# A 64-row score product run on 128 rows, with zero-padded copies of q, in an attention, gated-MLP and experts kernel

## The chip, the cores and the metric

The kernel runs on one core of one Trainium2 chip. The metric is the device time of one execution in microseconds (us); the median of three runs before the change is 1014.93 us (1014.54 to 1016.13). A core has a matrix engine (PE, with its weight loads listed apart as PEld), a vector engine (DVE), a scalar engine (ACT), a general engine (POOL) and an engine that here only issues DMA transfers (SP). Each works through its own instructions in order and waits on semaphores for the others.

## The reference

Three layers follow one another, on 8 batches of 576 tokens and a width of 512: an attention with pooled keys, a gated MLP with a spatial mixing, and four experts with a causal attention each, of which the two best per token are added up. The change is in the third layer, which per batch and expert computes:

```python
for e in range(E):                       # 4 experts, head size 64
    q = x @ wq[e]; k = x @ wk[e]; v = x @ wv[e]
    scores = scale * (q @ k.transpose(0, 2, 1))
    scores = np.where(causal, -1000000000.0, scores)
    scores = scores - scores.max(-1, keepdims=True)
    a = np.exp(scores)
    a /= a.sum(-1, keepdims=True) + 1e-09
    ye = a @ v @ wo[e]
    ...                                  # added with the gate's weight
```

## The kernel before, in words

**Precision.** Matrix products run in a reduced 32-bit format (F32R). To keep accuracy, an operand is split into a high part, which that format holds, and a low part, which is the rest; a product is the sum of high by high, low by high and high by low.

**Phases.** Class PhaseA runs the first two layers, batch by batch, until about 596 us of the trace; class PhaseB runs the experts from there to the end. PhaseB takes the four experts as two pairs per batch, p = 0 and p = 1, and I call the stretch of one pair a first half and a second half of the batch. One batch takes 50.6 us in the middle of the phase. Within a pair there are nine units, u = 0 to 8, in the order of QT (L598): unit 0 is the last 64 tokens of both experts together (e = 2), units 1 to 4 are the query blocks 3, 2, 1, 0 of the pair's first expert, and units 5 to 8 those of the second. Because of the causal mask their scores are 512, 384, 256 and 128 columns wide.

**One unit.** score() (L799) computes the scores in a PSUM bank; a DVE instruction applies the mask and takes the extremum (L825); ACT takes the exponential (L828); DVE makes the reciprocal of the sum (L839, L840); POOL or DVE scales the row (L844); PE transposes it (L870, in trans); ACT and DVE copy the transpose into high and low parts (L874, L875); av() multiplies by v (L890). The loop of run() (L943 on) emits score of unit k, scale of unit k - 1, some filling work, and the transposes of unit k - 3 (LAG = 3). The filling work is listed by unit in FILL, FIRSTF and LASTF: the next projections of q and k (proj, L691, with put_q and put_k), of v (vproj), loads of x, and the output products of the batch before (outp, L912 to L914). This code order sets the order on PE.

**The score products.** put_q (L704) lays q out so that one product does two thirds of the sum: qs[:, e] has the high part of expert e in one half of the 128 partitions and the low part in the other half, and kd (written by four DMAs per pair, L734) has the high part of k in both halves. L823 multiplies these on 128 rows. The third term, high q by low k, runs on the 64 rows of expert e alone:

```python
nc.tensor.matmul(o, qs[:, e, 128 * i:n], kd[:, e, :n], start=True, stop=False)                # L823
nc.tensor.matmul(o, qs[hi(e), e, 128 * i:n], kl[hi(e), :n], start=False, stop=True)           # L824
```

kl holds the low part of k, of the first expert in partitions 0 to 63 and of the second in 64 to 127. Unit 0 does the same third term on 128 rows, with qd, a matrix that is zero outside two diagonal blocks (L813).

**Order and buffers.** The tile framework derives all waits from reads and writes of the tiles, and orders the instructions of each engine. q and k have two sets of buffers, taken in turn by pair. All of PhaseB's loads, stores and copies by DMA are issued by SP in one order.

Of the kernel before, what the change touches and what calls it, by code (L numbers as in the profile page):

```python
# [8 lines left out]
F32 = mybir.dt.float32  # L9
F32R = mybir.dt.float32r  # L10
# [32 lines left out]
class PhaseA:  # L43
# [35 lines left out]
    def consts(self):  # L79
        nc, c = self.nc, self.c  # L80
        self.ident = c.tile([128, 128], F32, name="ident")
        make_identity(nc, self.ident)
        self.cm = c.tile([128, 8], F32, name="cm")
        nc.scalar.dma_start(self.cm, self.ins["cm"])
        self.kbd, self.vhi, self.vlo, self.vl1, self.vl2 = [], [], [], [], []
        for i in range(1):
            for n, sh, dt in (("kbd", [128, NP, 144], F32), ("vhi", [128, NP, 128], F32R), ("vlo", [128, NP, 128], F32R)):
                t = c.tile(sh, dt, name=f"{n}{i}")
                nc.gpsimd.memset(t.bitcast(F32) if dt == F32R else t, 0.0)
                getattr(self, n).append(t)  # L90
        self.mhalf = c.tile([128, 2], F32, name="mhalf")
        nc.gpsimd.memset(self.mhalf, -0.5)
        warm = c.tile([128, 2], F32, tag="wl", name="warm", bufs=2)
        nc.scalar.activation(warm, self.mhalf, AF.Exp)
        self.vn2 = c.tile([128, 512], F32R, name="vn2")
        nc.gpsimd.memset(self.vn2.bitcast(F32), 0.0)
        nc.gpsimd.memset(self.vn2[64:66].bitcast(F32), 1.0)
# [515 lines left out]
class PhaseB:  # L613
# [23 lines left out]
    def consts(self):  # L637
        nc, c, w = self.nc, self.c, self.w
        wt = [c.tile([128, 4112], F32R, tag="wi", name=n, bufs=2) for n in ("wqh", "wql")]
        self.wq = [t[:, :3088].rearrange("p (k n) -> p k n", k=4) for t in wt]  # L640
        self.wo = [t[:, 3088:].rearrange("p (k n) -> p k n", k=2) for t in wt]
        self.mk = c.tile([128, 640], F32, tag="kbd0", name="mk")
        nc.gpsimd.memset(self.mk, 0.0)
        nc.gpsimd.affine_select(self.mk[:, 448:576], self.mk[:, 448:576], pattern=[[-1, 128]], compare_op=OP.is_ge,
                                fill=NEG, base=0, channel_multiplier=1)
        for h in range(2):
            r = slice(64 * h, 64 * h + 64)
            nc.gpsimd.affine_select(self.mk[r, 576:], self.mk[r, 576:], pattern=[[-1, 64]], compare_op=OP.is_ge,
                                    fill=NEG, base=0, channel_multiplier=1)
        self.ml = bass.AP(tensor=self.mk.tensor, offset=self.mk.offset, ap=[list(self.mk.ap[0]), [192, 4], [1, 64]])  # L650
        self.tri = c.tile([128, 4, 4], F32, tag="st", name="tri", bufs=3)
        nc.gpsimd.memset(self.tri, 0.0)
        for e in range(1, 4):
            nc.gpsimd.memset(self.tri[:, e, :e], 1.0)
        warm = c.tile([128, 2], F32, tag="wl", name="warm", bufs=2)
        nc.scalar.activation(warm, self.ident[:, :2], AF.Exp)
        self.qs, self.lg = [], []
        for i in range(2):
            a = c.tile([128, 2048], F32R, tag="wo", name=f"qs{i}", bufs=2)
            t = a[:, :1280].rearrange("p (e n) -> p e n", e=2)  # L660
            nc.gpsimd.memset(t[:, 0, S:].bitcast(F32), 0.0)
            nc.gpsimd.memset(t[:, 1, 512:S].bitcast(F32), 0.0)
            d = a[:, 1280:1408]
            nc.gpsimd.memset(d.bitcast(F32), 0.0)
            self.qs.append((t, d, a[:, 1408:1984]))
        self.pr = c.tile([128, 5, S], F32, tag="pv", name="pr", bufs=2)
        self.sc = c.tile([128, 5, S], F32, tag="pv", name="scr", bufs=2)
        self.vts = [c.tile([128, 5, S], F32R, tag="ws", name=f"vt{i}", bufs=2) for i in range(2)]
        for i in range(2):
            t = c.tile([128, 5, 4], F32, name=f"lg{i}")  # L670
            nc.gpsimd.memset(t, 0.0)
            self.lg.append(t)
# [31 lines left out]
    def put_q(self, b, p, ps, h, s):  # L704
        nc = self.nc
        t, qd, _ = self.qs[(2 * b + p) % 2]
        A, C = slice(0, 64), slice(64, 128)
        n = HS if h == 0 else 512 - HS
        o = [(t[:, 1, h * HS:h * HS + n], ps[:, :n])]
        if h:  # L710
            o.append((t[:, 1, S:], ps[:, n:]))
        nc.scalar.activation(t[A, 0, s], ps[A], AF.Copy)
        for d, x in o:
            nc.scalar.activation(d[C], x[C], AF.Copy)
        nc.vector.tensor_sub(t[C, 0, s], ps[A], t[A, 0, s].bitcast(F32))
        for d, x in o:
            nc.vector.tensor_sub(d[A], x[C], d[C].bitcast(F32))
        if h:
            for e, r in enumerate((A, C)):
                nc.scalar.activation(qd[r, 64 * e:64 * e + 64], ps[r, n:], AF.Copy)  # L720
            self.QK["q", b, p] = (t, qd)

    def put_k(self, b, p, ps, h, s):
        nc, w = self.nc, self.w
# [74 lines left out]
    def score(self, b, p, u):  # L799
        nc, w = self.nc, self.w  # L800
        i, e = QT[u]
        qs, qd = self.QK["q", b, p]
        kd, kl = self.QK["k", b, p]
        hi = lambda e: slice(64 * e, 64 * e + 64)
        st = w.tile([128, 8], F32, name="sm", bufs=4)
        pt = self.pr[:, (18 * b + 9 * p + u) % 5]
        if e == 2:
            parts = []
            for s in (slice(0, 320), slice(320, S)):
                o = self.bank("s4")[:, :s.stop - s.start]  # L810
                nc.tensor.matmul(o, qs[:, 0, 512:], kd[:, 0, s], start=True, stop=False)
                nc.tensor.matmul(o, qs[:, 1, 512:], kd[:, 1, s], start=False, stop=False)
                nc.tensor.matmul(o, qd, kl[:, s], start=False, stop=True)  # L813
                parts.append((o, s))
            o = parts[1][0].rearrange("p (a n) -> p a n", a=4)
            nc.vector.tensor_tensor_reduce(o, o, self.ml, -0.125, BIG, OP.add, OP.min, st[:, 4:5])
            o = parts[0][0]
            nc.vector.tensor_tensor_reduce(o, o, self.mk[:, 0:1].to_broadcast([128, 320]), -0.125, st[:, 4:5],
                                           OP.add, OP.min, st[:, 0:1])
        else:  # L820
            n = 128 * i + 128
            o = self.bank("s")[:, :n]
            nc.tensor.matmul(o, qs[:, e, 128 * i:n], kd[:, e, :n], start=True, stop=False)  # L823
            nc.tensor.matmul(o, qs[hi(e), e, 128 * i:n], kl[hi(e), :n], start=False, stop=True)  # L824
            nc.vector.tensor_tensor_reduce(o, o, self.mk[:, 576 - n:576], -0.125, BIG, OP.add, OP.min, st[:, 0:1])  # L825
            parts = [(o, slice(0, n))]
        for j, (o, s) in enumerate(parts):
            nc.scalar.activation(pt[:, s], o, AF.Exp, bias=st[:, 0:1], scale=-1.0, accum_out=st[:, 1 + 4 * j:2 + 4 * j])  # L828
        self.U[b, p, u] = (pt, st)
# [170 lines left out]
```

## Time and profile before

| | us |
|---|---|
| median of three runs | 1014.93 |
| profiled execution, its time | 1014.54 |
| its span, from the first to the last instruction | 1012.8 |
| PE busy over the span | 955.0 (94%), 6488 products |
| DVE busy | 720.9 (71%) |
| ACT busy | 516.2 (51%) |
| POOL busy | 490.5 (48%) |
| L823, 128 products | 279 to 562 ns each in the record, median 404 |
| L824, 128 products | 322 to 579 ns each in the record, median 439 |

How to read it: consecutive products overlap in the records, since a product's record runs from its start until its last result is out. What a product costs PE is the step from its start to the start of the next one, and that is read from a timeline, not from the mean duration. The share of busy time is an average over a phase that has stretches of different kinds; so the rows below take single half batches and single instructions.

### The profile page before, as it was taken

What the parts mean: (1) busy time and instruction counts of PE and PEld (TensorE: products, weight loads), DVE (VectorE), ACT (ScalarE), POOL (GpSimd) and SP (SyncE); (2) the same over time, 40 slices, a digit from 0 to 9 for tenths busy, and PEclk for the clock granted to TensorE, in tenths of its full rate; (3) what the DMA queues carried; (4) which work ended last, traced back from release to release, by engine and by line L of the source; (5) the groups of instructions that cost most, each with busy time, mean ns of one, the idle gap of its engine ahead of it and who ended that gap; (6) DMA issues with size and microseconds to landing.
All of it is one profiled execution on the core that took longest, in us unless ns stands there. A gap on an engine that the chain in (4) does not pass through costs nothing.

```text
span 1012.8 us, 18277 instructions
## 1 busy us (share of the span) xinstructions
PE 955.0 (94%) x6488; PEld 871.6 (86%) x6488; DVE 720.9 (71%) x1901; ACT 516.2 (51%) x1291; POOL 490.5 (48%) x666
## 2 busy tenths in 40 slices
PE   4577899999999999999999998999999999999998
PEld 3466889989999899899998997989898989898987
DVE  6998747657477575674775238896969696969685
ACT  5575334243243342432433415766666666767676
POOL 6863638459377483692773603142424242424221
PEclk9589999999999999999999997999999999999999
DMA  9421302202213023032131122131313131312111
GB/s 328 175 98 45 124 36 79 104 23 72 111 34 125 36 78 115 11 95 89 40 111 38 37 67 71 28 106 36 107 36 106 37 106 37 106 37 71 36 48 71
DMA packets 35258, 78.72 MB, mean 78 GB/s; under 512 B 4448, under 2 KB 10592, under 8 KB 34272
## 3 DMA queue, kind: packets, MB, share of 16 engines
q1 hardware_dynamic: 35024, 77.55, 24.0%
q8 instruction: 52, 0.85, 0.4%
q14 instruction: 38, 0.31, 0.1%
q10 hardware_dynamic: 144, 0.00, 0.0%
HBM read 49.23 MB, written 18.87 MB: 67 GB/s over the span
## 4 chain that ended last, share of the span: by engine, by line
PE 68%; DVE 19%; ACT 4%; POOL 4%; issue 3%; DMA 1%; SPq 0%; POOLq 0%; DVEq 0%; ACTq 0%
PE pj L699 4%; PE av L890 4%; PE op L445 4%; PE t L870 3%; PE op L446 3%; PE op L447 3%; PE pj L701 3%; PE pj L700 3%; PE s L824 3%; PE sp L420 3%; PE sp L422 3%; PE sp L421 3%; PE sc L230 3%; DVE vnl L390 2%; DVE vnh L392 2%
## 5 line engine op out<-in xcount | busy, mean ns | idle before, releaser
L844 POOL TENSOR_SCALAR pr<-pr,sm,gw 128x128 f32<-128x128 f32 (+3 forms) x119 | 79.3, 667 | 175.6 <-DVE sm L840 125.5
L828 ACT ACTIVATE pr<-s,sm 128x256 f32<-128x256 f32 (+4 forms) x160 | 83.0, 520 | 35.4 <-DVE sm L825 17.5
L332 POOL TENSOR_TENSOR xu<-x 128x576 f32<-128x576 f32 x28 | 39.2, 1435 | 98.2 <-DVE x L327 85.4
L446 PE MATMUL op<-g,woh 128*128 128x288 f32 x256 | 76.7, 301 | 4.2 <-POOL g L433 3.8
L420 PE MATMUL sp<-wsh,vnh 128*128 128x288 f32 x256 | 78.3, 306 | 1.6 <-ACT vnh L388 1.6
L404 PE MATMUL up<-x,wih 128*128 128x288 f32 x256 | 76.9, 301 | 2.4 <-ACT vg L364 2.3
L699 PE MATMUL pj<-xbh,wqh 128*128 128x288 f32 x256 | 78.8, 308 | 0.0
L445 PE MATMUL op<-g,woh 128*128 128x288 f32 x256 | 78.3, 309 | 0.0
L421 PE MATMUL sp<-wsh,vnl 128*128 128x288 f32 x256 | 76.1, 297 | 0.0
L422 PE MATMUL sp<-wsl,vnh 128*128 128x288 f32 x256 | 75.9, 297 | 0.0
L406 PE MATMUL up<-x,wil 128*128 128x288 f32 x256 | 75.7, 296 | 0.0
L700 PE MATMUL pj<-xbl,wqh 128*128 128x288 f32 x256 | 75.4, 294 | 0.0
L701 PE MATMUL pj<-xbh,wql 128*128 128x288 f32 x256 | 75.3, 294 | 0.0
L405 PE MATMUL up<-x,wih 128*128 128x288 f32 x256 | 75.1, 293 | 0.0
L447 PE MATMUL op<-g,wol 128*128 128x288 f32 x256 | 74.9, 297 | 0.0
L825 DVE CUSTOM_DVE_ANT_0 s<-s,mk 128x512 f32<-128x512 f32 (+3 forms) x128 | 62.4, 488 | 6.9 <-PE s L824 6.7
L282 ACT ACTIVATE pth<-tr 128x640 fp32r<-128x640 f32 (+1 forms) x40 | 26.2, 655 | 78.5 <-PE tr L281 68.9
L870 PE MATMUL t<-ident,pr 128*128 128x128 f32 x320 | 60.9, 290 | 4.7 <-DVE pr L844 3.0
L875 DVE TENSOR_TENSOR pbl<-t,pbh 128x512 fp32r<-128x512 f32 (+3 forms) x128 | 60.7, 484 | 3.9 <-ACT pbh L874 1.9
L230 PE MATMUL sc<-kbd,qt 128*128 128x144 f32 (+1 forms) x320 | 49.7, 301 | 11.5 <-DMA qt<-q_in 9.2
L874 ACT ACTIVATE pbh<-t 128x512 fp32r<-128x512 f32 (+3 forms) x128 | 53.5, 440 | 10.4 <-PE t L870 8.7
L361 PE MATMUL vp<-wih,x 128*128 128x512 f32 x128 | 52.0, 406 | 6.3 <-ACT wih L128 5.0
(237 smaller groups left out, 3398.4 us busy)
## 6 DMA issues: line engine op xcount, KB each, us to landing
kraw<-k_in SPq DMA_DIRECT2D x16, 576.0 KB, 3.8
x<-x SPq DMA_DIRECT2D x32, 288.0 KB, 2.1
xb<-x SPq DMA_DIRECT2D x32, 288.0 KB, 2.9
kd<-scr SPq DMA_DIRECT2D x64, 144.0 KB, 2.5
out<-o SPq DMA_DIRECT2D x32, 288.0 KB, 2.2
vraw<-v_in SPq DMA_DIRECT2D x16, 512.0 KB, 4.1
qt<-q_in SPq DMA_DIRECT2D x7, 1152.0 KB, 6.9
st<-w_in_in SPq DMA_DIRECT2D x8, 512.0 KB, 8.5
```

What stands on the lines that cost most here:

```text
L230: nc.tensor.matmul(ps[:m, p // 2, (p % 2) * 144:(p % 2) * 144 + 144], qt[:, p, o:o + m], kbd[:, p, :], start=p % 2 == 0, stop=True, skip_g ...
L420: nc.tensor.matmul(o, vh[:, k, c], self.ws[0][:, k, s], start=k == 0, stop=False)
L421: nc.tensor.matmul(o, vl[:, k, c], self.ws[0][:, k, s], start=False, stop=False)
L422: nc.tensor.matmul(o, vh[:, k, c], self.ws[1][:, k, s], start=False, stop=False)
L445: nc.tensor.matmul(o, self.wo[0][:, k, c], gh[:, s], start=k == 0, stop=False)
L446: nc.tensor.matmul(o, self.wo[0][:, k, c], gl[:, s], start=False, stop=False)
L447: nc.tensor.matmul(o, self.wo[1][:, k, c], gh[:, s], start=False, stop=k == 3)
L699: nc.tensor.matmul(ps, self.wq[0][:, kc, c], xh[:, s], start=kc == 0, stop=False)
L700: nc.tensor.matmul(ps, self.wq[0][:, kc, c], xl[:, s], start=False, stop=False)
L701: nc.tensor.matmul(ps, self.wq[1][:, kc, c], xh[:, s], start=False, stop=kc == 3)
L828: nc.scalar.activation(pt[:, s], o, AF.Exp, bias=st[:, 0:1], scale=-1.0, accum_out=st[:, 1 + 4 * j:2 + 4 * j])
L870: nc.tensor.transpose(ps[:, j], pt[:, 128 * j:128 * j + 128], self.ident)
```

## The change

Four tiles qz of 128 partitions by 512 columns are added, two for each of the two buffer sets, in the space of PhaseA's constants vhi0, vlo0, vn2 and gln. One half of each (64 partitions) is set to zero once by POOL. put_q copies the high part of q of each expert into the other half by a DMA (two per pair, 32 in all). The third score product then takes qz[e] and all of kl on 128 rows. The sum is the same: the rows of the other expert are multiplied by zero.

```diff
@@ consts @@
+        self.qz = [[c.tile([128, 512], F32R, tag=g, name=f"qz{g}") for g in pair] for pair in (("vhi0", "vlo0"), ("vn2", "gln"))]
+        for pair in self.qz:
+            for e, z in enumerate(pair):
+                nc.gpsimd.memset(z[64 * (1 - e):64 * (1 - e) + 64].bitcast(F32), 0.0)
@@ put_q, if h @@
-            self.QK["q", b, p] = (t, qd)
+            qz = self.qz[(2 * b + p) % 2]
+            for e, r in enumerate((A, C)):
+                nc.sync.dma_start(qz[e][r].bitcast(F32), t[r, e, :512].bitcast(F32))
+            self.QK["q", b, p] = (t, qd, qz)
@@ score @@
-        qs, qd = self.QK["q", b, p]
+        qs, qd, qz = self.QK["q", b, p]
-        hi = lambda e: slice(64 * e, 64 * e + 64)
-            nc.tensor.matmul(o, qs[hi(e), e, 128 * i:n], kl[hi(e), :n], start=False, stop=True)
+            nc.tensor.matmul(o, qz[e][:, 128 * i:n], kl[:, :n], start=False, stop=True)
```

On PE the order stays as it was, instruction for instruction; so does that of DVE and ACT. Units 4 and 5 of a first half with the transposes between them, on PE, before (qs_5907 is the buffer set of first halves):

```order
L823 MATMUL s<-kd,qs_5907 128x128
L824 MATMUL s<-qs_5907 128x128
L870 MATMUL t<-ident,pr 128x128 x4
L823 MATMUL s<-kd,qs_5907 128x512
L824 MATMUL s<-qs_5907 128x512
L870 MATMUL t<-ident,pr 128x128 x3
```

The same place on PE now (line numbers are six higher):

```order
L829 MATMUL s<-kd,qs_5907 128x128
L830 MATMUL s<-qs_5907,qzvhi_5915 128x128
L876 MATMUL t<-ident,pr 128x128 x4
L829 MATMUL s<-kd,qs_5907 128x512
L830 MATMUL s<-qs_5907,qzvlo_5916 128x512
L876 MATMUL t<-ident,pr 128x128 x3
```

Only the operand of the third product has moved, from qs to qz; kl lies in the buffer set too, which is why qs stays in the row.

On SP, from the start of PhaseB (kd are the copies of k, xb loads of the next batch's x, out the results), before:

```order
L734 DMA kd<-scr 64x576 x8
L629 DMA xb<-x_1_58 128x576
L629 DMA xb<-x_2_59 128x576 x3
L734 DMA kd<-scr 64x576 x8
L629 DMA xb<-x_2_59 128x576
L629 DMA xb<-x_3_60 128x576 x2
L916 DMA out<-o 128x576 x2
```

SP from the same point now:

```order
L727 DMA qzvhi_5915<-qs_5907 64x512
L727 DMA qzvlo_5916<-qs_5907 64x512
L741 DMA kd<-scr 64x576 x4
L727 DMA qzvn_5917<-qs_5911 64x512
L727 DMA qzgln<-qs_5911 64x512
L741 DMA kd<-scr 64x576 x4
L629 DMA xb<-x_1_58 128x576
L629 DMA xb<-x_2_59 128x576 x3
```

The two copies of q stand directly ahead of the four copies of k of the same pair.

## Rows read from the trace of the kernel before

**Rows 1.** Engines by stretch: first halves of batches 0 and 4, second half of 4.
```profile
core 0: us, PE busy (x) PEld busy (x) DVE busy (x) ACT busy (x) POOL busy (x), PEclk, DMA share, GB/s
608.90:628.10 19.20, 15.17 (x87) 12.02 (x86) 16.61 (x63) 12.23 (x36) 5.83 (x7) 0.86 0.19 48
...
807.50:830.90 23.40, 23.12 (x156) 20.31 (x154) 21.33 (x77) 16.96 (x53) 12.03 (x15) 1.00 0.27 78
830.90:858.10 27.20, 27.17 (x193) 24.66 (x194) 19.32 (x77) 17.31 (x55) 6.65 (x11) 1.00 0.23 66
```

**Rows 2.** Timeline of PE (start, length, instruction), units 4 to 6, first half.
```profile
821.57 0.32 PE L824 MATMUL s<-qs 64*128 64x128 f32 x1
821.82 0.66 PE L870 MATMUL t<-ident,pr 128*128 128x128 f32 x4
822.23 0.47 PE L823 MATMUL s<-kd,qs 128*128 128x512 f32 x1
822.64 0.50 PE L824 MATMUL s<-qs 64*128 64x512 f32 x1
823.07 0.55 PE L870 MATMUL t<-ident,pr 128*128 128x128 f32 x3
...
824.36 0.39 PE L912 MATMUL op<-ah,wqh 128*128 128x256 f32 x1 [0.19 <-DVE scr L895]
```

**Rows 3.** Timeline of PE, last transposes of unit 5, then unit 0.
```profile
830.93 0.66 PE L870 MATMUL t<-ident,pr 128*128 128x128 f32 x4
831.35 0.39 PE L811 MATMUL s<-kd,qs 128*128 128x320 f32 x1
831.58 0.31 PE L812 MATMUL s<-kd,qs 128*128 128x320 f32 x1
831.72 0.31 PE L813 MATMUL s<-qs 128*128 128x320 f32 x1
831.87 0.28 PE L811 MATMUL s<-kd,qs 128*128 128x256 f32 x1
```

**Rows 4.** Timeline of PE, first products after an L824, second half.
```profile
836.39 0.39 PE L764 MATMUL vp<-wqh,xbh 128*128 128x260 f32 x1
836.62 0.28 PE L765 MATMUL vp<-wqh,xbl 128*128 128x260 f32 x1
836.74 0.28 PE L766 MATMUL vp<-wql,xbh 128*128 128x260 f32 x1
```

**Rows 5.** Timeline of the weight loads (PEld), that of one L824.
```profile
822.64 0.18 PEld L824 LDWEIGHTS s<-qs 64*128 64x128 f32 x1 [0.24 <-issue]
```

**Rows 6.** Engines by stretch, columns as in Rows 1, batch 4.
```profile
817.10:832.00 14.90, 14.59 (x98) 12.64 (x97) 14.49 (x48) 10.62 (x34) 9.69 (x12) 1.00 0.52 143
...
848.20:855.40 7.20, 7.20 (x49) 5.94 (x48) 6.58 (x22) 5.18 (x15) 0.74 (x3) 1.00 0.35 83
```

**Rows 7.** Timeline of DVE, waits for L824: batches 0, 4 and 7.
```profile
614.49 0.56 DVE L825 CUSTOM_DVE_ANT_0 s<-s,mk 128x384 f32<-128x384 f32 x1 [0.28 <-PE s L824]
...
817.07 0.57 DVE L825 CUSTOM_DVE_ANT_0 s<-s,mk 128x384 f32<-128x384 f32 x1 [0.53 <-PE s L824]
...
978.89 0.43 DVE L825 CUSTOM_DVE_ANT_0 s<-s,mk 128x256 f32<-128x256 f32 x1 [0.91 <-PE s L824]
```

**Rows 8.** Timeline of POOL, the scaling of two units 5.
```profile
829.44 1.44 POOL L844 TENSOR_SCALAR pr<-pr,sm,gw 128x512 f32<-128x512 f32 x1 [0.59 <-DVE sm L840]
...
855.21 0.77 POOL L844 TENSOR_SCALAR pr<-pr,sm,gw 128x512 f32<-128x512 f32 x1 [0.52 <-DVE sm L840]
```

**Rows 9.** Timeline of PE, transposes of unit 5 of a second half.
```profile
857.76 0.60 PE L870 MATMUL t<-ident,pr 128*128 128x128 f32 x4
858.12 0.39 PE L811 MATMUL s<-kd,qs 128*128 128x320 f32 x1
```

**Rows 10.** The page's DMA issues: the copies of k (KB, us to landing).
```profile
kd<-scr SPq DMA_DIRECT2D x64, 144.0 KB, 2.5
```

**Rows 11.** Timeline of POOL: the first memset of PhaseB and the wait before it.
```profile
594.80 0.15 POOL L661 MEMSET qs<- 128x64 f32 x1 [12.36 <-PE op L446]
```

## The prediction

> **What bounds the kernel now.** I read the busy time by stretch first. The change touches only the experts' phase, the last 411 us, and there the two halves of a batch differ. In a second half PE is busy 27.17 of 27.20 us and DVE 19.32, so PE sets the time. In a first half PE is busy 23.12 of 23.40 us and DVE 21.33 [rows 1]; both look full. A finer cut shows who leads: from 817.1 to 832.0 DVE is busy 14.49 of 14.90 us [rows 6], and PE waits for it, 0.19 us at L912 [rows 2], and again at 830.93, where the transposes begin as POOL's scaling (829.44 + 1.44) ends, which had itself waited for DVE's reciprocal [rows 8, 3]. DVE waited for PE once in that half, 0.53 us before L825 at 817.07 [rows 7]. So first halves run at DVE's pace from 817 on. Then I read steps on the timeline of PE, since records overlap.
>
> **What a 64-row product costs.** In unit 5 L823 starts at 822.23, L824 at 822.64 and the next transpose at 823.07: steps of 0.41 and 0.43 us for 512 columns [rows 2]. Full-row products step by 0.14 to 0.15 us for 320 columns (831.58, 831.72, 831.87), and by 0.23 where they come directly after transposes (831.35 to 831.58) [rows 3]. By proportion 512 columns want 0.145 x 512 / 320 = 0.23, and 0.09 more after transposes, 0.32. So L823 loses 0.41 - 0.32 = 0.09 us ahead of the 64-row product, and L824 itself 0.43 - 0.23 = 0.20. What follows loses too: the first product after an L824 steps 0.23 (836.39 to 836.62) where the next steps 0.12 [rows 4]: 0.11. Four transposes after an L824 take 0.41 (821.82 to 822.23) [rows 2], and 0.36 after a full-row product (857.76 to 858.12) [rows 9]: 0.05. The weight load says why: that of L824 starts at 822.64 with its own product, after 0.24 us of idle that no engine ends [rows 5]. It isn't loaded ahead, and what stands behind it isn't either.
>
> L813 is the form that the change gives to L824, zeros and low k on 128 rows, and it steps 0.15 us with no such gaps [rows 3]. I take that price for all widths. For 128 columns L824 steps 0.25 (821.57 to 821.82) [rows 2]; a full-row product of that width lies between 0.06 (by proportion) and 0.12 (the step for 260 columns [rows 4], were the load and not the columns the limit). I take 0.11, near the upper end, since the load has to fit in: 0.14 saved there. For 256 and 384 columns I take the 0.20 of 512.
>
> Here the Trainium skill speaks against the change. "TensorE: Matmul & The Clock Gate", Part 3 (Packing small matmuls), says that weight loads overlap running products only when their row groups differ, and its table in "Why this matters for your kernels" gives a single product on 32 rows the time of one on 128. By that L824 would save nothing on 128 rows, and the sum would be zero. Rows 2 and 3 differ from it, 0.43 us against 0.23 by proportion, so the sum goes by the rows.
>
> **The sum on PE.** A score followed by a filling product saves 0.09 + 0.20 + 0.11 = 0.40 us; one followed by transposes 0.34; one of 128 columns 0.06 less. By FILL, units 1, 2, 3, 7 and 8 of a second half have filling products: 4 x 0.40 + 0.34 (unit 8, 128 columns) + 0.28 (unit 4) + 2 x 0.34 = 2.90 us. In a first half these are units 1, 3 and 6: 3 x 0.40 + 3 x 0.34 + 2 x 0.28 = 2.78. Eight batches make 8 x 5.68 = 45.4 us of PE time. Not all reaches the end.
>
> **Second halves.** Between the wait at 830.93 and the next stretch that DVE leads stand units 1 to 7, 2.56 us. Is anything late in their place? DVE is busy 6.58 of 7.20 us from 848.2 to 855.4 [rows 6]. The tightest place I find is the transposes of unit 5 at 857.76 [rows 9]: POOL is done at 855.98 [rows 8], 1.78 us ahead, while PE comes 0.28 + 0.34 + 0.34 + 0.40 + 0.34 = 1.70 us sooner by units 4 to 8. That just holds. For a DVE that can't be squeezed by as much I take off 0.2 us. Seven second halves (batches 0 to 6) at 2.36 us: 16.5 us.
>
> **First halves.** Here PE gets 2.78 us and DVE no less work. DVE's one wait for PE goes: 0.53 us, of which six stand in the trace (batches 1 to 6, alike), 3.2 us. What is left of PE's gain turns into waits at L912 and at the transposes of unit 5. In batch 0 the wait is 0.28 us [rows 7], 0.3 saved. Bounds for first halves are 0 and 2.78 each.
>
> **Batch 7** has no next batch to project. Its DVE waits for L824 for 0.91 us at 978.89 [rows 7]; PE's 5.7 us is the upper bound, 0.9 the lower. I take 2.0, nearer to the row.
>
> **What is added.** 32 DMAs on SP, ahead of the copies of k and of the out stores and x loads behind them. A copy of k takes 2.5 us to land [rows 10], and one of q, 128 KB against 144, should be alike. In batch 4, q's last projection of the first half stands ahead of 817.1, and its first use is L824 of unit 1 in the second half, just before 836.39 [rows 4]: 19 us for 2.5. They wait for ACT's copy of the same q, and the copies of k behind them wait for a later projection, so nothing on SP is held back by much. The cover is gone only if ACT's copies came 15 us late. Four memsets on POOL: the nearest row is 0.15 us for 64 columns [rows 11], so up to 8 x 0.15 = 1.2 us each for 512, and PhaseB's first memset follows on 12.36 us of idle. Nothing for both, with up to 2 us for the start of the phase kept in the range.
>
> **The time.** 16.5 + 3.2 + 0.3 + 2.0 = 22.0 us. The profiled execution took 1014.54 us (span 1012.8 and 1.7 around it), so 992.5; the median of the three runs is 0.4 higher, and I predict 993 us.
>
> **Rivals.**
> - All PE time reaches the end, 1014.9 - 45.4 = 969.5 us. For it: PE is busy 23.12 of 23.40 us in a first half too [rows 1]. Against it: DVE's 14.49 of 14.90 us [rows 6]. Chance 0.05.
> - DVE's backlog spills over into second halves, and only half of their gain stays: 7 x 1.3 + 3.2 + 0.3 + 0.9 = 13.5, or less, 1001 to 1005 us. For it: the 0.1 us that is left at 857.76. Against it: DVE has 7.9 us idle in a second half. Chance 0.09.
> - The row count doesn't matter, as the skill's table has it, or a full-row third product steps like the 64-row one for another reason (kl's or q's place in memory): 1015 us. L813 speaks against it. Chance 0.03.
> - Slower: PE, with 2.2 us more of waits in each first half, loses its clock there. In batch 0, where PE was busy 15.17 of 19.20 us, the granted clock was 0.86, which is 5.4 us at 1.2 instead of 2.4 GHz; in batch 4, with 23.12 of 23.40, it was 1.00 [rows 1]. With the change PE would be busy some 20.3 of 22.9. Were the clock low for all of DVE's 14.9 us, 7.45 us of work would be lost, 2.2 of it in waits: 5.2 us in each of 7 first halves, 37 us, 1030 us. It decides from 3.1 us per half on (about 10.7 us at the low level), where it eats the 22. Against it: the new waits are shorter than batch 0's, and come between full stretches. Chance 0.05.
>
> **How the numbers follow.** The forecast has 0.78, and its own range is 984 to 999 us: down to it if first halves give 1.8 us each rather than 0.53, up if second halves lose another 0.8. The range of 8 in 10 is 981 to 1003 us: its lower end is half of the first halves' 2.78 and all of the second halves' 2.90 (11 + 23), its upper end most of the backlog rival. Differences within 0.2% (2 us) can't be told from no change here. Faster: forecast, both rivals that only change its size: 0.92. The same: 0.03. Slower: 0.05.
>
> **What would show it.** Third products at about 0.23 us for 512 columns, loads ahead of their products; a second half shorter by 2.3 to 2.6 us and a first half by 0.5; DVE without its 0.53 us wait; longer waits of PE at L912 and at the transposes of unit 5 of first halves. I am wrong in mechanism if the third product still steps 0.4 us, or if first halves shrink as much as second ones, and wrong in size if new waits stand in second halves or the clock falls in a middle batch.

## The result and the profile after

The changed kernel takes 986.46 us (median of four runs, 986.12 to 987.11) against 1014.73 us for the kernel before in the runs beside it: a ratio of 0.9723 [0.9706, 0.974], the 95% interval in brackets. That is 28.3 us faster; 22 were forecast, 993 us, with a range of 981 to 1003. The profiled execution has a span of 984.4 us where it was 1012.8.

I read it in the order of the prediction. The steps first: the timeline of PE (start, length, instruction), units 4 to 6 of the first half of batch 4, the place of [rows 2]:

```profile
805.36 0.28 PE L830 MATMUL s<-qs,qzvhi 128*128 128x128 f32 x1
805.48 0.62 PE L876 MATMUL t<-ident,pr 128*128 128x128 f32 x4
805.85 0.48 PE L829 MATMUL s<-kd,qs 128*128 128x512 f32 x1
806.17 0.39 PE L830 MATMUL s<-qs,qzvlo 128*128 128x512 f32 x1
806.40 0.49 PE L876 MATMUL t<-ident,pr 128*128 128x128 f32 x3
...
807.99 0.39 PE L918 MATMUL op<-ah,wqh 128*128 128x256 f32 x1 [0.75 <-DVE scr L901]
```

L829 now steps 0.32 us (805.85 to 806.17) where L823 stepped 0.41; L830 steps 0.23 (to 806.40) where L824 stepped 0.43; for 128 columns the third product steps 0.12, where it was 0.25. In return the wait at L918 has grown from 0.19 to 0.75 us. The products behind a third product, the place of [rows 4] and its column sizes:

```profile
819.51 0.39 PE L830 MATMUL s<-qs,qzvn 128*128 128x512 f32 x1
819.75 0.28 PE L771 MATMUL vp<-wqh,xbh 128*128 128x260 f32 x1
819.86 0.28 PE L772 MATMUL vp<-wqh,xbl 128*128 128x260 f32 x1
```

The first of them steps 0.11 us, like any other; it was 0.23. The loads, the place of [rows 5]:

```profile
805.83 0.19 PEld L829 LDWEIGHTS s<-kd,qs 128*128 128x128 f32 x1
805.94 0.19 PEld L830 LDWEIGHTS s<-qs,qzvlo 128*128 128x128 f32 x1
```

The weights of L830 are loaded at 805.94, 0.23 us before the product starts at 806.17, while L829 runs. L824's load started with its product.

The half batches, in the view of [rows 1]: both halves of batch 0, both of batch 4, and the stretch of the first half that answers to [rows 6]:

```profile
core 0: us, PE busy (x) PEld busy (x) DVE busy (x) ACT busy (x) POOL busy (x), PEclk, DMA share, GB/s
609.30:628.00 18.70, 13.20 (x92) 11.73 (x90) 16.66 (x65) 12.17 (x36) 5.86 (x7) 0.97 0.26 63
627.97:651.67 23.70, 23.65 (x179) 23.13 (x178) 21.12 (x84) 16.09 (x52) 5.18 (x8) 0.95 0.28 74
792.15:814.98 22.83, 21.34 (x161) 20.23 (x159) 21.60 (x84) 17.03 (x54) 12.57 (x17) 1.00 0.35 99
814.98:839.11 24.13, 24.13 (x192) 23.78 (x190) 18.31 (x71) 16.73 (x54) 5.86 (x10) 1.00 0.28 77
801.20:814.60 13.40, 11.91 (x88) 10.92 (x87) 12.98 (x41) 9.82 (x33) 9.24 (x11) 1.00 0.57 157
```

A second half is still full on PE (24.13 of 24.13 us) and shorter. A first half now leaves PE idle for 1.49 us of 22.83 and DVE busy for 21.60; in its second part DVE is busy 12.98 of 13.40 us. The granted clock is 1.00 in batch 4.

Where the time came from, by the start of unit 0 of each half (L811, now L817) to the next:

| stretch | before, us | after, us | saved in all |
|---|---|---|---|
| batch 0, first and second half | 19.95, 27.01 | 18.69, 23.70 | 4.2, with a start 0.4 later |
| batches 1 to 6, first halves | 23.8 each (23.62 to 23.80) | 22.8 (22.59 to 22.87) | 5.9 |
| batches 1 to 6, second halves | 26.76 | 24.03 (to 24.13) | 16.3 |
| batch 7, to the last product | 22.23, 27.61 | 20.42, 27.04 | 2.4 |
| after the last product | 3.9 | 4.3 | -0.4 |

That is the 28.4 us of the span. DVE's waits over the experts' phase (engine, line, waited for: us in all, times, longest), first before, then after:

```profile
DVE sm L839 <- ACT pr L828: 23.5, 35, 2.1
...
DVE s L825 <- PE s L824: 6.7, 16, 0.9
```

```profile
DVE sm L845 <- ACT pr L834: 16.0, 26, 1.2
```

The wait for the third product [rows 7] is gone from the list, and the one for ACT's exponential, which follows it by two steps, has lost 7.5 us as well. PE's waits after, batches 1 to 6:

```profile
PE op L918 <- DVE scr L901: 4.5, 6, 0.8
PE t L876 <- POOL pr L850: 3.4, 6, 0.6
```

Before, the first of these was 1.2 us over six times and the second did not show there. These are the two places the prediction named. In a second half the place of [rows 9] and [rows 8] stayed without a wait:

```profile
837.87 1.53 POOL L850 TENSOR_SCALAR pr<-pr,sm,gw 128x512 f32<-128x512 f32 x2 [0.52 <-PE t L876]
```

```profile
838.76 0.60 PE L876 MATMUL t<-ident,pr 128*128 128x128 f32 x4
```

The POOL row holds two scalings, of 0.77 us (512 columns) and 0.66 (384); the first, unit 5's, ends at 838.64, and the transposes start at 838.76. The margin is 0.1 us, as forecast.

### The profile page after: what moved, and what is told of

Its sections match the earlier page's. It is cut to its first block, busy times and chain, and to the rows that moved or that the text cites. A ratio compares the mean times of both kernels' runs of the same rounds, so it can differ in the third digit from the quotient of the medians.

```text
span 984.4 us, 18357 instructions
## 1 busy us (share of the span) xinstructions
PE 915.4 (93%) x6488; PEld 863.3 (88%) x6488; DVE 715.2 (73%) x1901; ACT 511.1 (52%) x1291; POOL 490.4 (50%) x670
## 4 chain that ended last, share of the span: by engine, by line
PE 57%; DVE 25%; ACT 8%; POOL 5%; issue 4%; DMA 1%; SPq 0%; POOLq 0%; ACTq 0%; DVEq 0%
PE op L445 4%; PE op L446 3%; PE op L447 3%; PE sp L420 3%; PE sp L422 3%; PE sp L421 3%; PE sc L230 3%; PE av L896 3%; DVE vnl L390 2%; DVE vnh L392 2%; ACT pr L834 2%; PE t L876 2%; PE tr L281 2%; DVE bs L376 2%; PE pj L705 2%
## 5 line engine op out<-in xcount | busy, mean ns | idle before, releaser
L703 PE MATMUL pj<-xbh,wqh 128*128 128x288 f32 x256 | 75.5, 295 | 0.0
L876 PE MATMUL t<-ident,pr 128*128 128x128 f32 x320 | 57.9, 280 | 9.4 <-POOL pr L850 6.0
L896 PE MATMUL av<-pbh,vt 128*128 128x320 f32 (+4 forms) x224 | 55.6, 278 | 2.4 <-ACT pbh L880 2.4
```

The source lines that it names most:

```text
L876: nc.tensor.transpose(ps[:, j], pt[:, 128 * j:128 * j + 128], self.ident)
L896: nc.tensor.matmul(ps[:, s - lo:], vt[:, j, 2 * p + e].rearrange("p a d -> p (a d)"), t[:, e, j * PTS + s:j * PTS + up], start=j == 0 and ...
```

## The experiments

Halves below are of batches 1 to 6, start of unit 0 to the next; the kernel before has 23.80 and 26.76 us, the changed one 22.83 and 24.03.

**E1: the new operand, on 64 rows.** Edit on the changed kernel; the tiles, their memsets and the 32 DMAs stay:

```diff
+            r = slice(64 * e, 64 * e + 64)
-            nc.tensor.matmul(o, qz[e][:, 128 * i:n], kl[:, :n], start=False, stop=True)
+            nc.tensor.matmul(o, qz[e][r, 128 * i:n], kl[r, :n], start=False, stop=True)
```

> All additions of the change stay (four memsets, 32 DMAs, q's copy as operand), but the third product runs on the 64 rows of its expert. Theory, the row count sets the step: it steps 0.43 us again for 512 columns, and the time is that of before, 1014.7 us within 2. Rival, what helped is where the operand lies or that it is a copy: about 986 us. Rival, the additions have a price that the gain hides: above 1016 us by that price.

Measured: 1014.61 us, ratio 1.0001 [0.9991, 1.001]; halves 23.80 and 26.76. At the place of [rows 2]:

```profile
822.19 0.47 PE L829 MATMUL s<-kd,qs 128*128 128x512 f32 x1
822.59 0.50 PE L831 MATMUL s<-qs,qzvlo 64*128 64x512 f32 x1
823.02 0.55 PE L877 MATMUL t<-ident,pr 128*128 128x128 f32 x3
```

The old steps, 0.40 and 0.43 us, are back. So the whole gain hangs on the row count; where q's copy lies gives nothing, and the memsets and DMAs cost nothing that can be measured.

**E2 and E3: full rows in one kind of half.** E1's edit with another r:

```diff
+            r = slice(0, 128) if p == 1 else slice(64 * e, 64 * e + 64)    # E2; E3 has p == 0
```

> The third product runs on 128 rows in second halves alone, on 64 in first halves. Theory, PE paces second halves and DVE first halves: seven second halves give 2.7 us each and the last 0.6, so 995 us. Rival, a saved step counts the same wherever it stands (half of 28 us): 1000.5 us.

> The third product runs on 128 rows in first halves alone. Theory, DVE paces them: 6 middle ones give about 1.0 us each, that of batch 0 1.2 and of batch 7 1.8, so about 1005.7 us. Rival, a saved step counts the same wherever it stands: 1000.5 us.

Measured: E2 996.11 us, 0.9825 [0.981, 0.9839], halves 23.80 and 24.03; E3 1006.51 us, 0.993 [0.9915, 0.9945], halves 22.75 and 26.78. Second halves give 18.5 us and first halves 8.1, together 26.6 of the 28.1 that E1 and the changed kernel lie apart. So the gains nearly add up, and the first halves' part is real: it does not come from second halves that end earlier.

**E4: the third product twice.** On the kernel before, executed once; the third term is added twice:

```diff
+            for x in range(2):
-            nc.tensor.matmul(o, qs[hi(e), e, 128 * i:n], kl[hi(e), :n], start=False, stop=True)
+                nc.tensor.matmul(o, qs[hi(e), e, 128 * i:n], kl[hi(e), :n], start=False, stop=x == 1)
```

> The kernel before with every 64-row third product issued twice on the same rows, so the scores hold the third term twice. Theory, the change between full and 64 rows costs: from the first to the second of the two the step is that of the columns, 0.23 us for 512, and only the second, ahead of full rows, steps 0.43. Rival, every 64-row product loads its weights late: both step 0.43. The second halves grow by 0.7 us (theory, 0.06 to 0.23 each of eight) or by 2.8 us (rival, 0.25 to 0.43 each).

Measured: 1031.55 us; halves 25.09 and 28.07. The timeline, where a pair of third products is one row:

```profile
838.07 0.36 PE L823 MATMUL s<-kd,qs 128*128 128x256 f32 x1
838.36 0.50 PE L825 MATMUL s<-qs 64*128 64x256 f32 x2
838.79 0.33 PE L871 MATMUL t<-ident,pr 128*128 128x128 f32 x1
```

The pair of 256 columns steps 0.43 us, where a single one steps 0.31 (median): the second costs its columns alone, 0.12. For 512 columns the pair steps 0.66 (medians 0.335 and 0.324) and a single one 0.42. So the extra 0.19 us is paid once for a pair of 64-row products, not by each of them; whether the change to 64 rows or the one back costs it isn't told apart, since each pair has both. I had expected it all on one of the two; it is spread over both. The weight loads of a pair of 384 columns, then the products:

```profile
832.15 0.29 PEld L825 LDWEIGHTS s<-qs 64*128 64x128 f32 x2 [0.19 <-issue]
```

```profile
832.15 0.62 PE L825 MATMUL s<-qs 64*128 64x384 f32 x2
832.70 0.39 PE L913 MATMUL op<-ah,wqh 128*128 128x256 f32 x1
```

The first load starts with its product, after 0.19 us of idle, as before; the second is done by 832.44, while the first product runs. A load is late where the row count changes, and not for 64 rows as such. My figure for the halves was added up wrongly, too: the medians give 0.24, 0.17, 0.12 and 0.11 us more for a pair of 512 to 128 columns, twice per half, 1.3 us, and 1.3 came. First halves grew by as much as second ones. Had DVE alone set their time, PE would have had room to take some of it in.

**E5 to E7: casts of x to ACT.** DVE's row for the second cast in a first half was long, 1.48 us, where others take 0.44, so I took work of that kind off DVE. x comes in four parts, kc = 0 to 3. E5 moves one cast per batch from batch 1 on, E6 (kc in (0, 1, 2, 3)) all four, both on the changed kernel; E7 is E5's edit on the kernel before:

```diff
-        nc.vector.tensor_copy(xh[:, :S], x)
+        if b > 0 and kc in (1,):
+            nc.scalar.activation(xh[:, :S], x, AF.Copy)
+        else:
+            nc.vector.tensor_copy(xh[:, :S], x)
```

> The changed kernel, with the cast of x's second part (one of four per batch, 1.48 us on DVE in a first half, where it runs beside POOL's subtraction) on ACT. Theory, DVE paces first halves and PE has 1.4 us of waits there (0.75 at L918, 0.61 at the transposes): six first halves give 1.0 to 1.4 us each, 978 to 980 us. Rival, another chain (ACT's exponential, POOL's scaling) holds them: 986 us or, by ACT's added 0.6 us, up to 990.

> The changed kernel, with all four casts of x per batch from the second batch on (2.85 us of DVE in a first half) on ACT. Theory: PE's waits of 1.4 us per first half are the most that can go, so at best 978 us, as with one cast, and ACT's 2.4 us more may give part of it back, 978 to 983. Rival, DVE alone decides: 2.85 us in each of six, 969 us.

> The kernel before, with the cast of x's second part on ACT as above (1.61 us of DVE there). Theory, in the kernel before first halves were near balance, PE's waits being 0.2 us at L912 and 0.3 at the transposes: 0.3 to 0.5 us in each of six, 1012 us. Rival, DVE alone paced them: 1.5 us each, 1005.5 us.

Measured: E5 989.57 us, 0.9753 [0.9739, 0.9768], halves 23.49 and 24.04; E6 985.71, 0.9722 [0.9706, 0.9738], 22.61 and 24.03; E7 1012.29, 0.9987 [0.9977, 0.9996], 23.57 and 26.77. E5 and E6 missed: with less work on DVE, one is 3 us slower than the changed kernel and the other no faster. E7 came out as expected in time, with 0.2 us per first half where I expected 0.3 to 0.5. First DVE, then POOL in E5:

```profile
806.24 1.56 DVE L633 CAST xbh<-xb 128x576 fp32r<-128x576 f32 x1
...
808.79 1.50 DVE L910 TENSOR_TENSOR al<-scr,ah 128x256 fp32r<-128x256 f32 x1 [0.29 <-ACT ah L909]
```

```profile
804.69 2.80 POOL L636 TENSOR_TENSOR xbl<-xb,xbh 128x576 fp32r<-128x576 f32 x2 [1.00 <-PE pj L707]
...
808.60 1.41 POOL L636 TENSOR_TENSOR xbl<-xb,xbh 128x576 fp32r<-128x576 f32 x1
```

POOL's subtractions of x, 1.4 us each, end at 807.49 (two back to back) and 810.01; DVE's cast ends at 807.80 and its subtraction of al (the low part of what the output products read), 0.54 us in the changed kernel, at 810.29. Both end 0.3 us after POOL. The casts and POOL in the changed kernel:

```profile
804.28 0.44 DVE L630 CAST xbh<-xb 128x576 fp32r<-128x576 f32 x1
...
805.48 1.48 DVE L630 CAST xbh<-xb 128x576 fp32r<-128x576 f32 x1
```

```profile
805.22 1.42 POOL L633 TENSOR_TENSOR xbl<-xb,xbh 128x576 fp32r<-128x576 f32 x1
```

POOL ends at 806.64, the cast at 806.96; the cast before it had no POOL subtraction beside it and took 0.44. So a DVE cast or subtraction on tiles in SBUF that starts beside POOL's subtraction is done only 0.3 us after that. One with an operand in PSUM isn't caught; in the changed kernel, first DVE, then POOL:

```profile
808.16 0.69 DVE L872 TENSOR_TENSOR pbl<-t,pbh 128x512 fp32r<-128x512 f32 x1
```

```profile
807.82 1.43 POOL L633 TENSOR_TENSOR xbl<-xb,xbh 128x576 fp32r<-128x576 f32 x1
```

That subtraction from the transposes in PSUM starts 0.34 us after POOL's, takes its usual 0.69 us and is done 0.4 us before it.

E5 also moved another cast than I meant. ACT's cast in E5:

```profile
804.32 0.68 ACT L631 ACTIVATE xbh<-xb 128x576 fp32r<-128x576 f32 x1
```

It stands in the place of the cast of 804.28, the one of 0.44 us; the cast that had been 1.48 us is still on DVE and takes 1.56. The cast of kc = 0 runs at the end of the half before, so that kc = 1 is the first of a half; E9 below, with kc = 0 and 1 on ACT, has ACT's casts at 801.22 and 812.00. In return al's subtraction, 0.54 us without the edit, is now caught and takes 1.50: POOL subtracts sooner, and the next DVE instruction is caught instead. To move the long cast alone was not tried. In E6 no cast is left to be caught, though al's subtraction is (1.30 us), and POOL's scaling of a score queues behind three subtractions. PE waits for that, six times over batches 1 to 6:

```profile
PE t L879 <- POOL pr L853: 9.6, 6, 1.7
```

The Trainium skill has a rule for this, "SBUF — State Buffer" (Who interferes with whom): a DVE copy, cast or tensor_scalar in a two-port mode, or a DVE instruction with two inputs in SBUF, shares ports with GpSimd, the whole instruction of the one that issues first goes ahead, and the other is blocked until then. The rows above agree with it: a cast and a two-input subtraction both ended 0.3 us after POOL.

**E8 to E10: the scaling that queues goes to DVE.** E8 is E6 with unit 2's scaling of first halves on DVE; E9 the same with two casts on ACT, kc in (0, 1); E10 is E8's edit on the kernel before:

```diff
-        (nc.vector if (p, u) in (SDF if b == 0 else SDL if b + 1 == B else ()) else
+        (nc.vector if (p, u) in (SDF if b == 0 else SDL if b + 1 == B else {(0, 2)}) else
```

> The kernel with all casts on ACT, and in batches 1 to 6 also unit 2's scaling of first halves on DVE instead of POOL. Theory, what held first halves after the casts had gone is POOL's order: that scaling stands behind three subtractions of x, and PE waited 1.56 us for it; without it 0.8 to 1.2 us go in each of six, 979 to 981 us. Rival, DVE's sum of work decides: 19.4 us of it plus 0.5 for the scaling, no change, 986 us.

> As the kernel with all casts on ACT and unit 2's scaling on DVE, but with only the first two casts of a batch on ACT. Theory, the last two (0.49 and 0.44 us on DVE, beside no subtraction) come after the tight stretch: the same within 2 us, 979 to 982 us. Rival, DVE's sum decides: 0.9 us more in each of six, 5 us above the one with all four.

> The kernel before (third product on 64 rows) with all casts on ACT and unit 2's scaling on DVE. Theory, with 64-row products PE is nearly full in first halves (waits of 0.5 us), so no more than 0.2 to 0.5 us go in each of six: 1011 to 1013 us. Rival, these edits shorten first halves by themselves: as much as on the changed kernel, 1 us or more each, 1008 us or less.

Measured: E8 983.70 us, 0.9695 [0.968, 0.9709], halves 22.22 and 24.19; E9 984.51, 0.9702 [0.9686, 0.9718], 22.40 and 24.03; E10 1009.76, 0.9952 [0.9937, 0.9967], first halves 23.13. E8 gained 2 us on E6, less than half of the 5 to 7 that I expected. E9 is the same as E8 within the 2 us expected, but not for the reason given: of the two casts left on DVE one is the long one (803.14, 1.54 us beside POOL), and its first halves are 0.2 us longer. First DVE, then POOL in E8:

```profile
803.94 1.34 DVE L853 TENSOR_SCALAR pr<-pr,sm,gw 128x384 f32<-128x384 f32 x1
```

```profile
802.26 2.80 POOL L636 TENSOR_TENSOR xbl<-xb,xbh 128x576 fp32r<-128x576 f32 x2 [0.99 <-PE pj L707]
```

The scaling, now on DVE, is caught as the cast was: 805.28 against 805.06. E10, between the two times expected of it, tells something else: its PE shows no wait in batches 1 to 6, so 23.13 us is what PE's work takes in a first half with the 64-row products. The kernel before, at 23.80, lay 0.67 us above that. Step by step in batch 4, the 0.67 stands in three places: 0.26 before L912, where the step is 0.63 us against 0.37; 0.21 in the steps of L912 to L914 behind it; and 0.19 before unit 5's transposes, 0.44 against 0.25. Only 0.28 of it showed as idle time, since a wait that is covered by the record of the product before doesn't show; so PE looked busy for 23.12 of 23.40 us there.

**E11 and E12: POOL's subtraction in four.** If DVE waits for the end of an instruction on POOL, a shorter instruction frees it sooner, with as much to subtract on POOL. E11, on the changed kernel; E12 is E8 with it:

```diff
-        eng.tensor_sub(xl, x, xh[:, :S].bitcast(F32))
+        for j in range(4 if b > 0 and eng is nc.gpsimd else 1):
+            s = slice(144 * j, 144 * j + 144) if b > 0 and eng is nc.gpsimd else slice(0, S)
+            eng.tensor_sub(xl[:, s], x[:, s], xh[:, s].bitcast(F32))
```

> The changed kernel, with POOL's subtraction of x (1.43 us, three per batch in first halves) in four pieces of 144 columns from the second batch on. Theory, DVE's casts and subtractions of SBUF data wait for the end of the POOL instruction that runs (a cast of 0.44 us took 1.48 beside it): in pieces the wait is at most one piece, 0.4 us, and 0.7 to 1.1 us go in each of six first halves, 980 to 982 us. Rival, the two slow each other however the work is cut: 986 us, or up to 3 us more by POOL's fixed cost of nine more instructions per batch.

> Casts on ACT, unit 2's scaling on DVE, and POOL's subtraction of x in four pieces. Theory: that scaling (1.34 us on DVE beside POOL) and the subtraction of the output's low part (0.85) fall to about 0.5 us each, and 0.8 to 1.0 us go in each of six first halves against the kernel without the pieces (983.7): 978 to 979 us. Rival, the two slow each other however the work is cut: 983.7 us.

Measured: E11 981.64 us, 0.9676 [0.966, 0.9693], halves 22.15 and 24.04; E12 980.68, 0.9666 [0.9651, 0.968], 21.45 and 24.27. First DVE, then POOL in E11:

```profile
802.40 0.74 DVE L630 CAST xbh<-xb 128x576 fp32r<-128x576 f32 x1
...
803.76 0.69 DVE L630 CAST xbh<-xb 128x576 fp32r<-128x576 f32 x1
...
804.37 0.71 DVE L909 TENSOR_TENSOR al<-scr,ah 128x256 fp32r<-128x256 f32 x1
```

```profile
800.97 1.86 POOL L635 TENSOR_TENSOR xbl<-xb,xbh 128x144 fp32r<-128x144 f32 x4 [1.05 <-PE pj L706]
...
803.64 2.24 POOL L635 TENSOR_TENSOR xbl<-xb,xbh 128x144 fp32r<-128x144 f32 x4
```

The casts now take 0.74 and 0.69 us, and POOL's subtraction takes longer, 1.86 and 2.24 us in four pieces against 1.43 in one. Two single pieces:

```profile
800.97 0.50 POOL L635 TENSOR_TENSOR xbl<-xb,xbh 128x144 fp32r<-128x144 f32 x1 [1.05 <-PE pj L706]
...
804.10 0.71 POOL L635 TENSOR_TENSOR xbl<-xb,xbh 128x144 fp32r<-128x144 f32 x1
```

The first four start 0.45 us apart, with no DVE cast or subtraction of al running when they start, so the 1.86 us are the price of four instructions. The second and third of the other four (0.71 and 0.67 us) start while such an instruction runs on DVE, and there POOL is held up too. The cut changes neither the order nor which engine does what, and gains 4.8 us. E12 gains 3.0 us on E8 and is the fastest, 34 us under the kernel before; it came out 1.7 us above what I expected.

## Why the prediction was right, and where it was off

**The mechanism was right.** A 64-row product between full-row ones costs 0.19 to 0.20 us over a full-row one (0.14 for 128 columns), 0.09 in the product ahead and 0.10 to 0.11 in a projection behind. Medians over all steps agree with the terms: L829 0.318 us for 512 columns (forecast 0.32), L830 0.23 (0.23), for 128 columns 0.11 (0.11), a projection of q or k behind 0.133 where it was 0.237. The first transpose behind went from 0.164 to 0.108, and in a group of four from 0.165 to 0.132, where 0.05 was taken. E1 shows that rows, not place, decide, and E4 that the extra comes where the row count changes.

**Second halves, 2.36 forecast, 2.73 measured.** The 0.2 us taken off for a DVE that can't be squeezed was not needed, and unit 8, which I left out as part of the stretch that DVE leads, gave its share too: 2.73 of PE's 2.90 us came. The medians of the steps that changed add up to 2.80, so most of what is missing was priced too high, as with unit 8's projection, which gave 0.05 instead of 0.11. The 0.37 us more than forecast are 2.2 us over batches 1 to 6. The rival of a backlog that spills over is out with it.

**First halves, 0.53 forecast, 0.97 measured.** Here a step failed: "Here PE gets 2.78 us and DVE no less work." DVE's instructions were as many, but two of its other waits depended on PE and on order in time. From the mask of the last unit of the half before to the reciprocal of unit 5 (batch 4, 807.07 to 829.08 before, 792.10 to 812.71 after) DVE took 1.40 us less: 0.53 by the wait I counted, about 0.34 by shorter waits for ACT's exponential, 0.34 by the first cast, which no longer runs beside POOL (0.78 to 0.44), and 0.13 by the second (1.61 to 1.48). 0.43 of it went back, since DVE starts that much later against unit 0 of PE. The remaining 0.06 I don't place. DVE's rows before:

```profile
808.29 0.15 DVE L839 TENSOR_SCALAR sm<-sm 128x1 f32<-128x1 f32 x1 [0.66 <-ACT pr L828]
...
820.32 0.78 DVE L630 CAST xbh<-xb 128x576 fp32r<-128x576 f32 x1
...
821.72 1.61 DVE L630 CAST xbh<-xb 128x576 fp32r<-128x576 f32 x1
```

The wait in the first of these is 0.30 us after the change:

```profile
792.98 0.16 DVE L845 TENSOR_SCALAR sm<-sm 128x1 f32<-128x1 f32 x1 [0.30 <-ACT pr L834]
```

So first halves of before did not run at DVE's pace in the sense that I used: by E10 they lay 0.67 us above PE's own work, and by E4 they grew with it in full. I read this as PE, ACT, DVE and POOL waiting for one another in a ring, so that a faster PE moved all of it; no run shows the ring by itself. What the prediction said of the rest held: after the change PE waits at L918 and at unit 5's transposes. What holds first halves back now is in part DVE behind POOL's subtraction, as E11 shows: cut it, and 0.7 us per half comes back. That is not all of it. The least step of each product, taken over all first halves of batches 1 to 6 with 128-row products, adds up to 20.4 us, an estimate of PE's own work there; the changed kernel's 22.8 lie 2.4 above it and E12's 21.45 still 1.0. What makes up the rest stays open.

**Batch 0, 2.7 forecast, 4.2 measured; batch 7, 2.0 and 2.4.** In batch 0 the clock stood at 1.2 GHz for 10.2 us (from 622.8) before and for 3.4 us (from 626.7) after; the granted clock of the first half rose from 0.86 to 0.97. PE had been busy for 2.76 of the 4 us ahead of it before, and for 1.18 of the 4 us ahead of it after. In the other runs such a stretch at that place was between 3.4 and 10.2 us long, also in E1, which has the steps of before and 6.8 us. How much of the 1.5 us is the change's own stays open. Halves of every kind saved more than forecast, so the total isn't near by errors that cancel; it is 6.3 us short, all to one side.

**Additions at nothing.** Right, by E1. The memsets took less than the 1.2 us each that I allowed, and ran at 541 to 583 us, before the experts' phase; the copies of q landed in 2.2 to 3.7 us, like those of k [rows 10], but a memset was 0.52 us where I had only one of 64 columns to go by [rows 11].

**The other rivals.** No effect of rows: out, by E1. By the Trainium skill's table in "TensorE: Matmul & The Clock Gate" (Why this matters for your kernels) E1 and the changed kernel would be alike; they are 28 us apart. Slower by the clock: PE now idles 1.49 us in a first half, and the granted clock stayed 1.00 in batches 1 to 6. All of PE's 45.4 us: out, 28.3 came.

## What to carry to other kernels

Look at the steps around a product that uses fewer rows than its neighbours, not at the product alone: if its operands can be padded with zeros to the same rows, the step of the product ahead and of the one behind shrink with it. Where two engines look equally full, don't give the gain of one to waits outright; look at which waits of the other hang on the first, directly or through a third engine. And where a vector instruction whose operands all lie in SBUF now and then takes three times its usual time, read what POOL ran beside it: moving work away may only move the collision, while cutting POOL's instruction frees the other engine sooner. Before you move one instruction of several alike, make sure from the trace which of them your edit takes.

## What the runs showed of the hardware

- The 0.19 us that a 64-row product between 128-row ones costs is paid once for two 64-row products in a row (E4: 0.66 us for a pair of 512 columns, 0.42 for one, 0.23 for a full-row one), and the second one's weights are loaded ahead.
- A DVE cast, scaling or subtraction with its tiles in SBUF that starts beside POOL's subtraction of x ended 0.2 to 0.3 us after it, four times in the rows of three traces (806.96 after 806.64, 807.80 after 807.49, 810.29 after 810.01, 805.28 after 805.06). How long it takes is then POOL's affair: 1.3 to 1.6 us instead of 0.4 to 0.6. A DVE subtraction that reads PSUM kept its 0.69 us beside it.
- Four pieces of such a subtraction took 1.86 us on POOL where one whole took 1.43, and 2.24 where two of them started beside a DVE cast or subtraction (0.7 us each instead of 0.5): POOL is held up by DVE as well, and the kernel gained all the same.
